# A recurrence, a mixture of experts and a feed-forward network in one kernel: the addition of an expert product's halves is issued one block later, and a split changes places with the next multiplication

## The chip, the core and the metric

The kernel runs on one core of one Trainium2 chip. The metric is device time in microseconds (us), from the first to the last instruction of one execution with what lies around it. The engines that matter here are PE (TensorE, the matrix multiplications, which write to the accumulators in PSUM), ACT (ScalarE), DVE (VectorE), POOL (GpSimd) and SP, whose queue issues most transfers (DMA). Each engine takes its own instructions strictly in the order in which the program lists them; between engines they wait for each other by semaphores.

## What is computed

Three layers follow each other. The reference, cut to what the change touches:

```python
x = attn_out.reshape(3072, 384)            # a complex linear recurrence over 768 steps (not touched)
# mixture of experts: each token goes to one of 8 experts
for e in range(8):
    h = np.maximum(x[mask] @ w1[e], 0.0)   # 384 -> 1024
    out[mask] = gate_w[mask, None] * (h @ w2[e])   # 1024 -> 384
# feed-forward network on all tokens
h = x @ w_in                               # 384 -> 2048
g = h * (1.0 / (1.0 + np.exp(-1.702 * h)))
y = g @ w_out                              # 2048 -> 384
```

## The kernel before

The matrix products run in 16-bit pieces: each operand is split into a rounded 16-bit half and the 16-bit rest ("split" below), and a product is the sum of three partial products (high by high, high by low, low by high) in one PSUM accumulator.

**The experts** (`moe`). The tokens are sorted by expert into 26 blocks of 128. The hidden dimension of 1024 is cut into NQ = 4 quarters of 256, and the program runs over the quarters q = 0 to 3 and in each over the 26 blocks, 104 steps in all. One step (q, b) issues in this order:

- `gemm1(q, b)`: six matmuls into one accumulator `ph` (three buffers), 512 columns wide; its two column halves hold parts of the same product and have to be added. ACT copies the right half to the tile `h` (L1083, three buffers), and DVE adds the left half to it (L1084): the addition of the halves.
- `late(2)`: `turn` of the block two steps back (q, b-2). PE transposes its `h` into the accumulator `pt` (L1090, two buffers), ACT takes the positive part of it as the high half of `hT` (L1093), DVE makes the low half (L1094), and that frees `pt`. Then `gemm2` of the block four steps back: six matmuls into `py` (L1105), which DVE adds to `acc` (L1112; L1110 in the first quarter).
- a share of two background jobs, each cut into steps. `halves` loads and splits the weights of the quarter after (while quarter 0 runs, those of quarter 1, and so on): ACT scales and rounds them (L997, L999, L1002), POOL subtracts (L1000), in quarter 0 also DVE (L1004). `narrow` turns the last layer's 64-bit weights into two 16-bit halves, from quarter 1 on, 32 weight blocks in all: six steps a weight block, with DVE in most (L946, L947, L950, L961, L964, L967), ACT in one (L957), and a transfer of the result (wh<-w, L970) that has to be through before the next L957 may write the same tile.

In quarter 0 each step also transposes and splits the next token block (`split`, L1068 to L1070).

So with n the number of the step, PE's row of work is gemm1(n), turn(n-2), gemm2(n-4), gemm1(n+1). PE's turn(n-2) needs two things of DVE: the addition of block n-2, and the low half of block n-4, which frees `pt`. Both stand next to each other in DVE's row, first the addition, then the low half.

**The end of the experts.** After the last step the remaining blocks are taken out in pairs, mixed with the first steps of the next layer (`begun`).

**The feed-forward network** (`Ffn`). Six tiles t of 512 tokens. `up` runs over f = 0 to 15 (NF = 16): nine matmuls into the accumulator `fph` (L1289, three buffers), then ACT's sigmoid (L1292) and DVE's multiplication with it (L1293), which frees `fph` and gives the hidden value; then the split of the value before, f-1: ACT's copy to 16 bit (L1296) and the subtraction of it (L1298), on DVE, and for t < 3 with f divisible by 3 on POOL. `down` multiplies with the second weight matrix (L1309) and is issued for the first time after three `up`s: the order is up 0, up 1, up 2, down 0, up 3, down 1, up 4, down 2, up 5, down 3, down 4, down 5. Beside `up` run `prep` of the next tile (squares L1232, a few small DVE steps, transposes L1256, splits L1260 and L1261) and in the first tiles the rest of `narrow`, by 1.5 steps an f in tile 0, 2 in tile 1, 2.5 in tile 2.

Of the kernel before, what the change touches and what calls it, by code (L numbers as in the profile page):

```python
# [16 lines left out]
AF = mybir.ActivationFunctionType  # L17
# [991 lines left out]
def moe(tc, cst, rt, wp, st, we, yd, lo, hi, x, psum, w0=None, w64=None, wh=None, ffn=None):  # L1009
# [3 lines left out]
    with ExitStack() as c2:  # L1013
# [58 lines left out]
        def gemm1(q, b):  # L1072
            w = ws[q]
            if b not in reg:
                reg[b] = nc.tensor.value_load(rt.eid[0:1, b:b + 1], min_val=0, max_val=E - 1)
            e = reg[b]
            ph = ph_.tile([P, 2 * FQ], F32, tag="ph", name=f"ph{q}_{b}")
            for k in range(KD):
                o = k * 2 * FQ
                nc.tensor.matmul(ph, lhsT=xT[:, b - lo, 0, k, :], rhs=w[:, e, o:o + 2 * FQ], start=k == 0, stop=False)  # L1080
                nc.tensor.matmul(ph[:, :FQ], lhsT=xT[:, b - lo, 1, k, :], rhs=w[:, e, o:o + FQ], start=False, stop=k == KD - 1)  # L1081
            h = wk.tile([P, FQ], F32, tag="h", name=f"h{q}_{b}", bufs=3)
            nc.scalar.copy(h, ph[:, FQ:])  # L1083
            nc.vector.tensor_tensor(out=h, in0=ph[:, :FQ], in1=h, op=ALU.add)  # L1084
            return h

        def turn(q, b, h):
            pt = pt_.tile([P, KD, P], F32, tag="pt", name=f"pt{q}_{b}")
# [31 lines left out]
                pass  # L1120
        gen = iter(())
        split(lo)
        hs, hTs = [], []
        NP = 2 * F2 // P
        fw, done, loaded = [], [], []
        conv = begun = iter(())
# [15 lines left out]

        def late(n):
            while len(hs) > n:
                q, b, h = hs.pop(0)
                hTs.append((q, b, turn(q, b, h)))
            while len(hTs) > n:
                gemm2(*hTs.pop(0))

        for q, b in seq:  # L1150
# [11 lines left out]
            if q == 0 and b > lo:  # L1162
                split(b + 1)
            hs.append((q, b, gemm1(q, b)))
            if q == 0 and b == lo:
                split(b + 1)
            late(LAG)
# [24 lines left out]
        late(LAG // 2)  # L1192
        next(begun, None)
        while hs:
            q, b, h = hs.pop(0)
            hTs.append((q, b, turn(q, b, h)))
        next(begun, None)
# [3 lines left out]
class Ffn:  # L1201
# [77 lines left out]
    def up(s, t, x, gT, tmp):  # L1279
# [3 lines left out]
        for f in range(s.NF + 1):  # L1283
            if f < s.NF:
                ph = s.ph.tile([P, T], F32, tag="ph", name=f"fph{t}_{f}")
                i = 0
                for k in range(KD):
                    for a, b in ((0, 0), (0, 1), (1, 0)):
                        nc.tensor.matmul(ph, lhsT=s.wi[f][:, a, k, :], rhs=xT[b][:, k], start=i == 0, stop=i == 3 * KD - 1)  # L1289
                        i += 1  # L1290
                h = tmp[f % 3]
                nc.scalar.activation(h, ph, AF.Sigmoid, scale=sig)  # L1292
                nc.vector.scalar_tensor_tensor(out=h, in0=ph, scalar=GS, in1=h, op0=ALU.mult, op1=ALU.mult)  # L1293
            if f:
                h = tmp[(f - 1) % 3]
                nc.scalar.copy(gT[:, f - 1, 0], h)  # L1296
                e = nc.gpsimd if t < 3 and f % 3 == 0 else nc.vector
                e.tensor_tensor(out=gT[:, f - 1, 1], in0=h, in1=gT[:, f - 1, 0], op=ALU.subtract)  # L1298
            yield

    def down(s, t, x, gT, tmp):
# [373 lines left out]
```

## Time and profile before

| | us |
|---|---|
| three runs, median | 966.82 (962.73 to 970.6) |
| the profiled execution | 961.36, with a span of 959.5 from the first to the last instruction |
| recurrence and routing | 0 to about 295 of the span |
| experts, quarter 0 | about 295 to 365 |
| experts, quarters 1 and 2 | about 365 to 490 |
| experts, quarter 3 and the end | about 490 to 558 |
| feed-forward network | about 553 to the end; its weights' conversion ends at about 650, PE ends at 938 |

Busy over the span: PE 881.4 us (92%), DVE 627.7 (65%), ACT 533.8 (56%), POOL 265.0 (28%). The granted clock was 0.985 on average and 1.00 between 374 and 662 us.

How to read it: PE is busy nearly throughout, so what counts is its idle time and what ended it. A row of the list of waits says which instruction waited, for which engine and line, how long in total, how often and at most. A row of the timeline gives start and duration in us, the engine, the line, the operation, the tiles written and read, the shape, and in brackets the engine's idle time before it with what ended it.

### The profile page before, as it was taken

What the parts mean: (1) busy time and instruction counts of PE and PEld (TensorE: products, weight loads), DVE (VectorE), ACT (ScalarE), POOL (GpSimd) and SP (SyncE); (2) the same over time, 40 slices, a digit from 0 to 9 for tenths busy, and PEclk for the clock granted to TensorE, in tenths of its full rate; (3) what the DMA queues carried; (4) which work ended last, traced back from release to release, by engine and by line L of the source; (5) the groups of instructions that cost most, each with busy time, mean ns of one, the idle gap of its engine ahead of it and who ended that gap; (6) DMA issues with size and microseconds to landing.
All of it is one profiled execution on the core that took longest, in us unless ns stands there. A gap on an engine that the chain in (4) does not pass through costs nothing.

```text
span 959.5 us, 17255 instructions
## 1 busy us (share of the span) xinstructions
PE 881.4 (92%) x5980; PEld 576.4 (60%) x5980; DVE 627.7 (65%) x1378; ACT 533.8 (56%) x1053; POOL 265.0 (28%) x215
## 2 busy tenths in 40 slices
PE   2789998999977999988999989989999999999994
PEld 0678877888965666555556644435545556456662
DVE  4887989887876898988998669996063170440000
ACT  7898776876645886765753456765063360440000
POOL 1330444136405663433520123223110101001110
PEclk9899999999988999999999999999999999999998
DMA  7532432220824755645637332121010000000000
GB/s 262 174 132 68 150 124 64 97 84 19 275 75 122 203 162 156 203 128 176 207 120 224 116 125 74 59 84 31 28 42 9 26 1 17 17 10 25 25 25 20
DMA packets 40403, 94.99 MB, mean 99 GB/s; under 512 B 6545, under 2 KB 19346, under 8 KB 40306
## 3 DMA queue, kind: packets, MB, share of 16 engines
q1 hardware_dynamic: 35138, 77.87, 25.1%
q0 software_dynamic: 4736, 14.69, 5.1%
q8 instruction: 56, 0.92, 0.4%
q10 hardware_dynamic: 432, 1.18, 0.4%
q14 instruction: 41, 0.34, 0.1%
HBM read 74.84 MB, written 18.81 MB: 98 GB/s over the span
## 4 chain that ended last, share of the span: by engine, by line
PE 44%; DVE 13%; DMA 4%; issue 3%; ACT 3%; POOL 0%; DVEq 0%; POOLq 0%; ACTq 0%; SPq 0%
PE fpo L1309 19%; PE fph L1289 12%; PE py L1105 5%; PE ph L1080 4%; DMA wh<-w 3%; PE ph L1081 2%; DVE w L961 2%; DVE x L1293 2%; DVE acc L1112 2%; DVE h L1084 1%; PE pt L1090 1%; DVE hT L1094 1%; DVE w L967 1%; DVE w L964 1%; PE px L1068 1%
## 5 line engine op out<-in xcount | busy, mean ns | idle before, releaser
L1289 PE MATMUL fph<-fx,fw 128*128 128x512 f16 x864 | 192.2, 379 | 6.4 <-DVE x L1293 6.3
L1293 DVE SCALAR_TENSOR_TENSOR x<-fph,x 128x512 f32<-128x512 f32 x96 | 65.9, 688 | 129.8 <-ACT x L1292 128.1
L1289 PEld LDWEIGHTS <-fw 128*128 128x128 f16 x864 | 84.5, 98 | 104.9 <-issue 9.5
L1309 PE MATMUL fpo<-fw,gT 128*128 128x384 f16 x768 | 125.3, 326 | 0.0
L1105 PE MATMUL py<-w,hT 128*128 x624 | 118.0, 326 | 1.3
L1080 PE MATMUL ph<-w,x 128*128 x312 | 108.1, 381 | 2.1 <-DVE w L1536 1.9
L1313 ACT ACTIVATE x<-fpo,fsm 128x384 f32<-128x384 f32 x24 | 13.9, 581 | 167.5 <-PE fpo L1309 167.5
L1309 PEld LDWEIGHTS <-gT 128*128 128x128 f16 x768 | 75.1, 98 | 49.9
L1292 ACT ACTIVATE x<-fph,fsm 128x512 f32<-128x512 f32 x96 | 65.6, 685 | 50.4 <-PE fph L1289 37.4
L1000 POOL TENSOR_TENSOR w<-ws,w 128x768 f16<-128x768 f32 x40 | 68.2, 1705 | 85.3 <-ACT w L999 80.6
L1314 POOL DMA_INDIRECT out<-x,fto x24 | 23.2, 965 | 245.3 <-ACT x L1313 245.3
L1081 PE MATMUL ph<-w,x 128*128 x312 | 85.4, 274 | 2.6 <-DVE x L1070 2.5
L1105 PEld LDWEIGHTS <-hT 128*128 128x128 f16 x624 | 60.9, 98 | 32.7 <-issue 4.1
L1083 ACT COPY h<-ph 128x256 f32<-128x256 f32 x104 | 38.5, 370 | 57.9 <-PE ph L1081 52.9
L1309 PE MATMUL fpo<-fw,x 128*128 128x384 f16 x384 | 62.7, 326 | 0.0
L1084 DVE TENSOR_TENSOR h<-ph,h 128x256 f32<-128x256 f32 x104 | 43.5, 418 | 26.7 <-ACT h L1083 25.8
L518 PE MATMUL pt<-c,f 128*96 128x128 f32 x384 | 53.1, 280 | 6.6 <-DVE f L492 4.8
L1309 PEld LDWEIGHTS <-x 128*128 128x128 f16 x384 | 37.6, 98 | 25.0
L536 PE MATMUL pt<-zq,zk 96*128 96x128 f32 x384 | 50.3, 278 | 0.7 <-ACT zk L526 0.7
L518 PEld LDWEIGHTS pt<-c,f 128*96 128x96 f32 x384 | 42.3, 129 | 13.5 <-DVE f L492 8.0
L1080 PEld LDWEIGHTS <-x 128*128 128x128 f16 x312 | 30.6, 98 | 31.4 <-issue 2.4
L1090 PE MATMUL pt<-c,h 128*128 128x128 f32 x208 | 40.6, 277 | 8.8 <-DVE hT L1094 8.6
(238 smaller groups left out, 1762.0 us busy)
## 6 DMA issues: line engine op xcount, KB each, us to landing
ws<-in_we SPq DMA_DIRECT2D x61, 384.0 KB
w<-in_w SPq DMA_DIRECT2D x32, 384.0 KB
qk<-in_qk SPq DMA_DIRECT2D x6, 1152.0 KB
yd<-acc SPq DMA_DIRECT2D x26, 192.5 KB
xd<-row SPq DMA_DIRECT2D x6, 589.5 KB
ar<-in_ar SPq DMA_DIRECT2D x6, 576.0 KB
ai<-in_ai SPq DMA_DIRECT2D x6, 576.0 KB
v<-in_v SPq DMA_DIRECT2D x6, 576.0 KB
```

Source lines behind the costliest of these rows:

```text
L518: nc.tensor.transpose(pt[:2 * D, h, :], T[FF][:, k, j * H + 4 * i + h].rearrange("p i d -> p (i d)"), cst["ident"])
L536: nc.tensor.matmul(ps[:, h - 4 * i, :], lhsT=T[ZK][:, h, :], rhs=T[ZQ][:, h, :], start=True, stop=True)
L1000: nc.gpsimd.tensor_tensor(out=wv[:, :, 1, :], in0=sv, in1=wv[:, :, 0, :], op=ALU.subtract)
L1080: nc.tensor.matmul(ph, lhsT=xT[:, b - lo, 0, k, :], rhs=w[:, e, o:o + 2 * FQ], start=k == 0, stop=False)
L1081: nc.tensor.matmul(ph[:, :FQ], lhsT=xT[:, b - lo, 1, k, :], rhs=w[:, e, o:o + FQ], start=False, stop=k == KD - 1)
L1084: nc.vector.tensor_tensor(out=h, in0=ph[:, :FQ], in1=h, op=ALU.add)
L1090: nc.tensor.transpose(pt[:, j, :], h[:, j * P:(j + 1) * P], cst["ident"])
L1105: nc.tensor.matmul(py, lhsT=hT[:, hl, j, :], rhs=w[:, e, o + off:o + off + DM], start=i == 0, stop=i == n - 1)
L1289: nc.tensor.matmul(ph, lhsT=s.wi[f][:, a, k, :], rhs=xT[b][:, k], start=i == 0, stop=i == 3 * KD - 1)
L1292: nc.scalar.activation(h, ph, AF.Sigmoid, scale=sig)
L1293: nc.vector.scalar_tensor_tensor(out=h, in0=ph, scalar=GS, in1=h, op0=ALU.mult, op1=ALU.mult)
L1309: nc.tensor.matmul(po, lhsT=gT[:, f, a, g * P:(g + 1) * P], rhs=s.wo[f][:, b, :], start=i == 0, stop=i == 3 * s.NF - 1)
```

## The change

Two edits. In `gemm1` the addition of the halves is no longer issued; accumulator and tile go to a list `whole`, and a new function `add` issues the addition of the oldest entry. The step calls it after the next block's `gemm1`, before `late`. Where a block would be transposed before that, `add` is called first. In `Ffn.up` the split of f-1 now stands ahead of the sigmoid and the multiplication of f.

```diff
@@ gemm1
             nc.scalar.copy(h, ph[:, FQ:])
+            whole.append((ph, h))
+            return h
+
+        def add():
+
+            ph, h = whole.pop(0)
             nc.vector.tensor_tensor(out=h, in0=ph[:, :FQ], in1=h, op=ALU.add)
-            return h
@@ late
             while len(hs) > n:
+                if len(whole) == len(hs):
+                    add()
                 q, b, h = hs.pop(0)
                 hTs.append((q, b, turn(q, b, h)))
@@ the step
             hs.append((q, b, gemm1(q, b)))
+            if len(whole) > 1:
+                add()
@@ the end of moe
         while hs:
+            if len(whole) == len(hs):
+                add()
             q, b, h = hs.pop(0)
             hTs.append((q, b, turn(q, b, h)))
@@ Ffn.up
-                h = tmp[f % 3]
-                nc.scalar.activation(h, ph, AF.Sigmoid, scale=sig)
-                nc.vector.scalar_tensor_tensor(out=h, in0=ph, scalar=GS, in1=h, op0=ALU.mult, op1=ALU.mult)
             if f:
                 h = tmp[(f - 1) % 3]
                 nc.scalar.copy(gT[:, f - 1, 0], h)
                 e = nc.gpsimd if t < 3 and f % 3 == 0 else nc.vector
                 e.tensor_tensor(out=gT[:, f - 1, 1], in0=h, in1=gT[:, f - 1, 0], op=ALU.subtract)
+            if f < s.NF:
+                h = tmp[f % 3]
+                nc.scalar.activation(h, ph, AF.Sigmoid, scale=sig)
+                nc.vector.scalar_tensor_tensor(out=h, in0=ph, scalar=GS, in1=h, op0=ALU.mult, op1=ALU.mult)
             yield
```

The rows of PE, POOL and SP are the same before and after; only those of DVE and ACT change. The line numbers of the changed kernel differ: there the addition is L1090, the low half of `hT` L1099, the sum into `acc` L1117, the copy of the split L1304, its subtraction L1306, the sigmoid L1309, the multiplication L1310.

First place: DVE in quarter 2, around block 20 (`h_20` is the block's tile, `hT_18` the low half of block 18, `w_13` and `w_14` are tiles of `narrow`). Before:

```order
L961 SCALAR_TENSOR_TENSOR w_14_6998<-w_14_6900,w_14_6998 128x384
L1084 TENSOR_TENSOR h_20_7042<-ph_20_7035,h_20_7042 128x256
L1094 SCALAR_TENSOR_TENSOR hT_18_7048<-pt_18_7045,hT_18_7048 128x256
L1112 SCALAR_TENSOR_TENSOR acc_4377<-py_16_7051,rs_4379,acc_4377 128x384
L964 SCALAR_TENSOR_TENSOR w_13_7029<-w_13_6902,w_13_7029 128x384
L967 SCALAR_TENSOR_TENSOR w_14_6998<-w_14_6900,w_14_6998 128x384
L1084 TENSOR_TENSOR h_21_7071<-ph_21_7064,h_21_7071 128x256
L1094 SCALAR_TENSOR_TENSOR hT_19_7077<-pt_19_7074,hT_19_7077 128x256
```

After:

```order
L961 SCALAR_TENSOR_TENSOR w_14_6997<-w_14_6899,w_14_6997 128x384
L1090 TENSOR_TENSOR h_19_7010<-ph_19_7003,h_19_7010 128x256
L1099 SCALAR_TENSOR_TENSOR hT_18_7047<-pt_18_7044,hT_18_7047 128x256
L1117 SCALAR_TENSOR_TENSOR acc_4377<-py_16_7050,rs_4379,acc_4377 128x384
L964 SCALAR_TENSOR_TENSOR w_13_7028<-w_13_6901,w_13_7028 128x384
L967 SCALAR_TENSOR_TENSOR w_14_6997<-w_14_6899,w_14_6997 128x384
L1090 TENSOR_TENSOR h_20_7041<-ph_20_7034,h_20_7041 128x256
L1099 SCALAR_TENSOR_TENSOR hT_19_7076<-pt_19_7073,hT_19_7076 128x256
```

The addition of block 20 has moved from ahead of the low half of block 18 to behind it, the sum into `acc` and this step's share of `narrow`.

Second place: DVE at the end of the experts (`h_25` is the last block's tile, `fx` belongs to the next layer). Before:

```order
L1084 TENSOR_TENSOR h_25_7934<-ph_25_7927,h_25_7934 128x256
L1094 SCALAR_TENSOR_TENSOR hT_23_7940<-pt_23_7937,hT_23_7940 128x256
L1112 SCALAR_TENSOR_TENSOR acc_4377<-py_21_7943,rs_4379,acc_4377 128x384
L1261 SCALAR_TENSOR_TENSOR fx_1_7635<-fpt_2_7920,fsi_7741,fx_0_7634 128x512
L1094 SCALAR_TENSOR_TENSOR hT_24_7957<-pt_24_7954,hT_24_7957 128x256
L1112 SCALAR_TENSOR_TENSOR acc_4377<-py_22_7960,rs_4379,acc_4377 128x384
L1112 SCALAR_TENSOR_TENSOR acc_4377<-py_23_7969,rs_4379,acc_4377 128x384
L1094 SCALAR_TENSOR_TENSOR hT_25_7981<-pt_25_7978,hT_25_7981 128x256
```

After, from the same low half of block 23 on:

```order
L1099 SCALAR_TENSOR_TENSOR hT_23_7939<-pt_23_7936,hT_23_7939 128x256
L1117 SCALAR_TENSOR_TENSOR acc_4377<-py_21_7942,rs_4379,acc_4377 128x384
L1272 SCALAR_TENSOR_TENSOR fx_1_7634<-fpt_2_7919,fsi_7740,fx_0_7633 128x512
L1099 SCALAR_TENSOR_TENSOR hT_24_7956<-pt_24_7953,hT_24_7956 128x256
L1117 SCALAR_TENSOR_TENSOR acc_4377<-py_22_7959,rs_4379,acc_4377 128x384
L1117 SCALAR_TENSOR_TENSOR acc_4377<-py_23_7968,rs_4379,acc_4377 128x384
L1090 TENSOR_TENSOR h_25_7933<-ph_25_7926,h_25_7933 128x256
L1099 SCALAR_TENSOR_TENSOR hT_25_7981<-pt_25_7978,hT_25_7981 128x256
```

The addition of block 25 now stands behind the sums of blocks 22 and 23, right ahead of the low half of its own block.

Third place: DVE in tile 1 of the feed-forward network, from f = 3 to f = 6 (the subtractions are the rows that write `gT`; that of f = 5 is on POOL). Before:

```order
L1293 SCALAR_TENSOR_TENSOR x<-fph_3_8382,x 128x512
L946 TENSOR_SCALAR w_25_8399<-w_25_8342 128x384
L947 TENSOR_SCALAR w_25_8399<-w_25_8399 128x384
L950 TENSOR_SCALAR w_25_8399<-w_25_8399 128x384
L1293 SCALAR_TENSOR_TENSOR x<-fph_4_8404,x 128x512
L1298 TENSOR_TENSOR gT_8024<-x,gT_8024 128x512
L1236 TENSOR_REDUCE fsm_8337<-fsm_8337 128x1
L961 SCALAR_TENSOR_TENSOR w_25_8399<-w_25_8342,w_25_8399 128x384
L964 SCALAR_TENSOR_TENSOR fw<-w_24_8344,fw 128x384
L1293 SCALAR_TENSOR_TENSOR x<-fph_5_8422,x 128x512
L1298 TENSOR_TENSOR gT_8024<-x,gT_8024 128x512
L967 SCALAR_TENSOR_TENSOR w_25_8399<-w_25_8342,w_25_8399 128x384
```

After, from the same row on:

```order
L1310 SCALAR_TENSOR_TENSOR x<-fph_3_8382,x 128x512
L946 TENSOR_SCALAR w_25_8399<-w_25_8342 128x384
L947 TENSOR_SCALAR w_25_8399<-w_25_8399 128x384
L950 TENSOR_SCALAR w_25_8399<-w_25_8399 128x384
L1306 TENSOR_TENSOR gT_8024<-x,gT_8024 128x512
L1310 SCALAR_TENSOR_TENSOR x<-fph_4_8404,x 128x512
L1247 TENSOR_REDUCE fsm_8337<-fsm_8337 128x1
L961 SCALAR_TENSOR_TENSOR w_25_8399<-w_25_8342,w_25_8399 128x384
L964 SCALAR_TENSOR_TENSOR fw<-w_24_8344,fw 128x384
L1306 TENSOR_TENSOR gT_8024<-x,gT_8024 128x512
L1310 SCALAR_TENSOR_TENSOR x<-fph_5_8422,x 128x512
L967 SCALAR_TENSOR_TENSOR w_25_8399<-w_25_8342,w_25_8399 128x384
```

Each subtraction on DVE now stands ahead of the multiplication that it followed; on ACT, in the same way, the copy of f-1 stands ahead of the sigmoid of f, where it stood behind it.

## Rows read from the trace of the kernel before

**Rows 1.** Waits of PE: who waited, for whom: us in total, times, longest us.
```profile
PE pt L1090 <- DVE hT L1094: 8.6, 10, 1.9
PE fph L1289 <- DVE x L1293: 6.3, 7, 1.6
```

**Rows 2.** Timeline, quarters 0 to 3: gemm2 of three steps on PE.
```profile
365.59 1.14 PE L1105 MATMUL py<-w,hT 128*128 x6
367.76 1.14 PE L1105 MATMUL py<-w,hT 128*128 x6
...
487.29 0.97 PE L1105 MATMUL py<-w,hT 128*128 x5
```

**Rows 3.** Stretches: length, then busy us of PE, PEld, DVE, ACT, POOL, granted clock.
```profile
374.00:432.00 58.00, 54.09 (x337) 32.92 (x336) 52.50 (x115) 40.70 (x87) 27.60 (x16) 1.00 0.53 166
594.00:625.00 31.00, 29.78 (x144) 14.02 (x143) 29.84 (x64) 23.26 (x45) 9.26 (x9) 1.00 0.28 86
```

**Rows 4.** Timeline, quarter 2, after ACT had waited for weights: ACT, DVE.
```profile
439.72 0.35 ACT L1083 COPY h<-ph 128x256 f32<-128x256 f32 x1
439.97 0.39 ACT L1093 ACTIVATE hT<-pt 128x256 f16<-128x256 f32 x1
...
440.11 0.42 DVE L1084 TENSOR_TENSOR h<-ph,h 128x256 f32<-128x256 f32 x1 [3.84 <-ACT h L1083]
```

**Rows 5.** Timeline, quarter 2, the last of the ten waits for pt: DVE, PE.
```profile
483.82 0.41 DVE L1094 SCALAR_TENSOR_TENSOR hT<-pt,hT 128x256 f16<-128x256 f32 x1
...
484.15 0.60 DVE L1112 SCALAR_TENSOR_TENSOR acc<-py,rs,acc 128x384 f32<-128x384 f32 x1
484.29 0.44 PE L1090 MATMUL pt<-c,h 128*128 128x128 f32 x2 [0.80 <-DVE hT L1094]
...
484.68 0.90 DVE L964 SCALAR_TENSOR_TENSOR w<-w,w 128x384 f16<-128x384 f32 x1
...
485.50 0.55 DVE L967 SCALAR_TENSOR_TENSOR w<-w,w 128x384 int32<-128x384 int32 x1
...
485.97 0.41 DVE L1084 TENSOR_TENSOR h<-ph,h 128x256 f32<-128x256 f32 x1
...
489.23 0.38 PE L1090 MATMUL pt<-c,h 128*128 128x128 f32 x2
```

**Rows 6.** Timeline, end of the experts: the last transposition and the sum behind gemm2.
```profile
553.42 0.38 PE L1090 MATMUL pt<-c,h 128*128 128x128 f32 x2
553.62 0.62 DVE L1112 SCALAR_TENSOR_TENSOR acc<-py,rs,acc 128x384 f32<-128x384 f32 x1 [0.32 <-PE py L1105]
```

**Rows 7.** Timeline, ACT in tile 0 of the feed-forward network: copy, then sigmoid.
```profile
572.21 0.61 ACT L1296 CAST x<-x 128x512 f16<-128x512 f32 x1
...
572.72 0.69 ACT L1292 ACTIVATE x<-fph,fsm 128x512 f32<-128x512 f32 x1
```

**Rows 8.** Timeline, tile 1, multiplications of f = 3 to 6 on DVE, one copy.
```profile
602.68 0.68 DVE L1293 SCALAR_TENSOR_TENSOR x<-fph,x 128x512 f32<-128x512 f32 x1
...
604.71 0.68 DVE L1293 SCALAR_TENSOR_TENSOR x<-fph,x 128x512 f32<-128x512 f32 x1
605.31 0.68 DVE L1298 TENSOR_TENSOR gT<-x,gT 128x512 f16<-128x512 f32 x1
605.42 0.62 ACT L1296 CAST gT<-x 128x512 f16<-128x512 f32 x1 [0.28 <-DVE x L1293]
...
606.91 0.69 DVE L1293 SCALAR_TENSOR_TENSOR x<-fph,x 128x512 f32<-128x512 f32 x1
...
608.58 0.69 DVE L1293 SCALAR_TENSOR_TENSOR x<-fph,x 128x512 f32<-128x512 f32 x1
```

**Rows 9.** Chain of work that ended last, tile 5: sixteen times nine matmuls.
```profile
821.34 31.08 PE fph L1289 x144
```

**Rows 10.** Timeline, one step of narrow on DVE beside a subtraction on POOL, and without.
```profile
592.65 1.15 POOL L1298 TENSOR_TENSOR x<-x 128x512 f16<-128x512 f32 x1 [4.56 <-ACT x L1296]
592.82 1.39 DVE L961 SCALAR_TENSOR_TENSOR w<-w,w 128x384 int32<-128x384 int32 x1
...
600.08 0.55 DVE L961 SCALAR_TENSOR_TENSOR w<-w,w 128x384 int32<-128x384 int32 x1
```

**Rows 11.** Timeline, PE's waits at the start and the end of tile 1.
```profile
597.75 1.46 PE L1289 MATMUL fph<-fx,fw 128*128 128x512 f16 x6 [0.78 <-DVE x L1293]
...
625.77 0.59 PE L1289 MATMUL fph<-fx,fw 128*128 128x512 f16 x2 [0.21 <-DVE x L1293]
```

More of the change, by code (lines that the diff above doesn't have):

```diff
@@ L1122, in moe @@
         split(lo)
-        hs, hTs = [], []
+        hs, hTs, whole = [], [], []
         NP = 2 * F2 // P
```

## The prediction

> **What bounds the kernel now.** I read PE's waits first, then the stretches in which they lie, then single steps of the timeline, and the chain of work last. PE is busy 92% of the span, so a change can only move what PE waits for. Two of its waits touch the edits [rows 1]: the transposition's accumulator `pt`, released by DVE's low half of `hT` (8.6 us, ten waits), and the feed-forward accumulator `fph`, released by DVE's multiplication (6.3 us, seven waits). The first lies in quarters 1 and 2: a step of PE takes 2.17 us (367.76 − 365.59), and 49 steps lie between the first and the last of the three rows, so 49 × 2.17 = 106.3 us would do and 121.7 went: 15.4 us were lost there [rows 2]. In that time DVE is nearly as busy as PE, 52.5 of 58 us against 54.1, ACT 40.7; in tile 1 of the feed-forward network DVE has 29.84 of 31 us against PE's 29.78 [rows 3]. So these are the two stretches where DVE's order decides. In tile 5, with no `narrow` beside it, PE runs on its own: 31.08 us for 16 f, 1.94 us an f [rows 9]. I expect nothing from the recurrence, quarter 3 and tiles 3 to 5.
>
> **Edit 1, the addition one block later.** It removes no instruction. What it could free is DVE: the addition waits for ACT's copy (3.84 us of idle ahead of it in one place), and what stands behind it in DVE's row waits as well. But right behind it stands the low half of `hT`, and that needs ACT's positive part, which stands right behind the same copy in ACT's row [rows 4]. There the copy starts at 439.72, the addition at 440.11; the positive part ends at 440.36, so without the addition in front the low half could start at about 440.40, against about 440.45 behind it (start to start of the pair in [rows 5]: 484.15 − 483.82 = 0.33). The gain is some 0.05 us an event. I count 0.
>
> What it costs: PE's turn(n−2) needs the addition of that block and, for `pt`, the low half of the block two before. Before, both stood side by side in DVE's row. Now the addition comes a DVE step later, behind the low half, the sum into `acc` and that step's `narrow`. At the last of the ten waits [rows 5] the low half ends at 484.23 and PE starts at 484.29. DVE then does the sum (to 484.75), L964 (to 485.58), L967 (to 486.05) and the next addition (to 486.38); in the new order that slot holds the addition this turn needs. So it starts at about 486.38 + 0.06 = 486.44 instead of 484.29, 2.15 us later. A part comes back: from 484.29 to the turn two steps on (489.23) went 4.94 us where two periods are 4.34. The 0.60 was paid by two turns that had to wait, 0.30 each. After the change only the first of them is late, and I take 2.15 − 0.30 = **+1.8 us**. I count it once, not per wait: when DVE and ACT come to a place in these quarters is set by their own work and by transfers that do not move, so each wait's release moves by the same step and PE is behind by the same amount all the way. Bounds: 0, if PE still had a step in hand; +0.85 if only the sum and the addition (0.52 + 0.33, start to start) lie between; +3.2 if a slow step of `narrow` lies between (L961 took 1.39 beside POOL, 0.55 alone [rows 10]; 2.15 + 0.84 = 3.0, and 0.2 more).
>
> In quarter 0 I count 0. There DVE's split of the next token block stands just ahead of the addition, and PE's next `gemm1` needs that split already; the turn stands behind this `gemm1`, which covers the 0.33 us of the addition. Without that cover it would be one step, 2.2 us, once.
>
> At the end of the experts the addition of block 25 now stands behind the sums of blocks 22 and 23. The last of these ends at 553.62 + 0.62 = 554.24 [rows 6]; 0.33 for the addition and 0.05 for the signal give 554.62. The last turn started at 553.42: **+1.2 us**, between 0.9 and 1.4, as nothing else is left on PE ahead of it.
>
> **Edit 2, the split ahead of the multiplication.** Write M(f) for the multiplication, S(f) for the subtraction. Before, ACT's sigmoid of f needed only PE, and the copy of f−1 came behind it. Now sigmoid(f) stands behind copy(f−1), which needs M(f−1), and M(f) needs sigmoid(f). That is a closed chain from one multiplication to the next: M 0.69, signal 0.03 (605.39 to 605.42 [rows 8]), copy to sigmoid 0.51 from start to start, sigmoid 0.69 [rows 7], signal 0.03: 1.95 us, against PE's 1.94. On its own that is harmless. But DVE in tiles 0 to 2 doesn't work evenly: it falls behind on f's with much `narrow` and catches up on light ones, and the chain is now a floor under the light ones.
>
> Tile 1 shows the cycle of three [rows 8]: 602.68 to 604.71 is 2.03 us, to 606.91 2.20, to 608.58 1.67; together 5.90, or 1.97 an f, just above PE's 1.94. In the new order the work between two multiplications is another: each S on DVE slides ahead of its M, 0.6 us. The f with `narrow`'s three steps gets 2.03 + 0.60 = 2.63, the next stays at 2.20, and the light f, whose S is on POOL, keeps 0.60 + 0.47 = 1.07 us of DVE work, but the chain holds it at 1.96. The cycle takes 2.63 + 2.20 + 1.96 = 6.79 instead of 5.90: 0.89 us idle on DVE per light f. Between PE's two waits at 597.75 and 625.77 [rows 11] lie 28.0 us or 14 f, with four or five cycles; the three `fph` buffers and DVE's own waits on PE take up some, and I count three: 3 × 0.89 = **+2.7 us**. In tile 0 the first wait finds an S of 0.6 ahead of its M, and `prep`'s squares on ACT come between copy and sigmoid and stretch the chain: **+1.5** (0 to 2). In tile 2 `narrow` gives DVE more work every f than the chain takes: **+0.3**. Together +4.5, between 0 and +7 (5 cycles in tile 1, 2 in tile 0 and half a microsecond in tile 2). In tiles 3 to 5 chain and PE differ by 0.01 to 0.02 us an f, 0.3 a tile, which the buffers hide.
>
> **A gain that the new order could give.** POOL's subtraction began beside DVE's L961, and this took 1.39 us where 0.55 is usual [rows 10]. After the swap POOL's subtraction starts about half a microsecond behind M(f−1)'s end and lies beside the next multiplication, which reads PSUM and one tile in SBUF. I counted six long steps of this kind between 562 and 650 us; six times 0.84 is 5 us of DVE time at most. I left it out of the sum since the L961 lies at the same place in the row and may meet POOL's conversions instead.
> The Trainium skill, *SBUF — State Buffer*, section "Who interferes with whom", says that a DVE instruction with two SBUF inputs contends with a GpSimd instruction that reads SBUF, because they share a read port, and that one with at most one SBUF input does not. L961 has two such inputs, so the rows agree; by the rule alone the multiplication would not suffer and the second rival below gains weight.
>
> **Sum.** 1.8 + 1.2 + 4.5 = +7.5 us. The profiled execution took 961.36, so 968.9; the median of the three runs lies 5.5 us above that execution (966.82), hence **974.3 us**.
>
> **Rivals.**
> - *Only the experts pay* (+3.0, 969.8 us): the feed-forward network breaks even, as the freed contention pays for the floor. For it: S done while DVE would wait, and the 0.84 us of [rows 10]. Against it: DVE has only 1.2 us of 31 idle in tile 1 [rows 3], so there is little waiting to fill.
> - *Faster*: the seven waits for `fph` vanish because POOL's subtraction no longer meets L961. −6.3 + 1.2, with edit 1 otherwise neutral: 966.82 − 5.1 = 961.7 us. It decides if copy(f−1) is done before PE ends f, so that sigmoid(f) never waits; against it stands that M(f−1) itself is late where PE waits.
> - *Worse, a new wait*: turn(n−1) now needs the addition at the head of the DVE step that comes right behind the low half of block n−3, so a two-step loop closes over turn, positive part, low half, sum, `narrow`, addition: 0.44 + 0.39 + 0.41 + 0.52 + 0.33 + two steps of `narrow` (0.9 + 0.5) = 3.5 of 4.34 us. With a slow `narrow` step (+0.84) it is full, and then each of the ten waits grows by up to 1 us beside terms above at their upper ends: +12 to +18, about 982 us.
> - *Nothing measurable*: buffers cover both edits, 966.8 us.
>
> **How the numbers follow.** Chances: forecast (+5 to +12, 972 to 979) 0.48; only the experts 0.20; faster 0.12; worse 0.12; nothing 0.08. The range goes from 965, which leaves out most of the faster case, to 982, which leaves out half of the worse one. One per cent, 9.7 us, is about what a measurement of this kernel can tell from no change. Above 976.5 lie the worse case and a third of the forecast (0.12 + 0.16, and 0.02 of the rest): slower 0.30. Below 957.2 only a part of the faster case: 0.03. Within 1%: 0.67.
>
> **What would show it.** Right, step by step: PE's waits for `pt` are released by the addition of DVE (tile `h`) instead of `hT`, and are larger in total; the gemm2 that stood at 487.29 lies about 1.8 us further from the one at 365.59; the last turn of the experts waits about 1.2 us for an addition behind a sum into `acc`; in tiles 0 to 2 the waits for `fph` grow from 6.3 to about 11 us, and DVE idles before multiplications on ACT's sigmoid in light f's, whose 1.67 us become about 1.96. Wrong: `fph` waits that shrink while sigmoids wait for nothing (the faster case); waits for `pt` that grow by far more than 2 us in total, with the addition as releaser at most of them (the worse case); a stretch of tiles 3 to 5 that gets longer, which no step here allows for.

## The result, and the profile after

The changed kernel takes 975.76 us (median of four runs, 971.35 to 979.42), the kernel before 967.87 (four runs): ratio 1.0104, 95% interval 1.0061 to 1.0147, so 6 to 14 us slower. The prediction said 974.3, in a range of 965 to 982. The profiled execution took 971.35 with a span of 969.6; the old one had 961.36 and 959.5, so it is 10.0 us longer (10.1 from span to span) where the sum said 7.5. Executions of one kernel spread over some 10 us, and in the traces most of this lies ahead of the experts, where no edit reaches (step 26 of the table below begins between 368 and 379 us), which is why the table counts from that step.

PE's waits in the changed kernel (who waited, for whom: us in total, times, longest us), against 8.6 and 6.3 in [rows 1]:

```profile
PE pt L1095 <- DVE h L1090: 14.4, 13, 3.8
PE fph L1300 <- DVE x L1310: 7.8, 9, 1.9
PE fpt L1267 <- DVE fx L1272: 1.5, 3, 0.5
```

The turns now wait for the addition (tile `h`) instead of the low half, and for 5.8 us more (1.0 of them is the last turn of the experts). The waits for `fph` have grown by 1.5 only; 1.5 us of waits for the next tile's preparation are new.

To see where the time goes I follow one instruction through all kernels: ACT's positive part behind the turn of step n (n counts the 104 steps; 26 is the first of quarter 1, 52 of quarter 2, 103 the last). Its start at steps 26 and 74, before and after (timeline: start, duration, engine, line):

```profile
370.19 0.38 ACT L1093 ACTIVATE hT<-pt 128x256 f16<-128x256 f32 x1
...
489.70 0.39 ACT L1093 ACTIVATE hT<-pt 128x256 f16<-128x256 f32 x1
```

```profile
369.18 0.38 ACT L1098 ACTIVATE hT<-pt 128x256 f16<-128x256 f32 x1
...
492.98 0.39 ACT L1098 ACTIVATE hT<-pt 128x256 f16<-128x256 f32 x1
```

From 26 to 74 went 119.51 us before and 123.80 after: 4.29 us lost in quarters 1 and 2, where the prediction had 1.8. In the same way the first sigmoid of a tile gives the loss in the feed-forward network; the column "tile 1" is thus what tile 0 has cost. One execution of each kernel, us behind the kernel before, counted from step 26 (steps) and from step 103 (tiles); "long steps" are DVE steps of `narrow` of over 1 us in quarters 1 and 2:

| kernel | step 52 | 53 | 74 | 103 | tile 1 | tile 2 | tile 3 | long steps |
|---|---|---|---|---|---|---|---|---|
| before | 0 | 0 | 0 | 0 | 0 | 0 | 0 | 8 |
| changed | 3.9 | 2.5 | 4.3 | 6.3 | 1.3 | 4.7 | 4.6 | 12 |
| e1 edit 1 alone | 4.3 | 2.9 | 5.9 | 7.1 | 0.0 | 0.0 | 0.1 | 13 |
| e2 edit 2 alone | -0.1 | -0.3 | -0.3 | -0.3 | 1.3 | 4.7 | 4.7 | 9 |
| e3 DVE half of edit 2 | -0.5 | -0.8 | 0.9 | 0.9 | 0.2 | 3.3 | 3.6 | 10 |
| e4 ACT half of edit 2 | -0.3 | -0.3 | 0.7 | 0.7 | 3.7 | 5.0 | 6.9 | 9 |
| e5 behind the low half | 0.1 | 0.1 | 3.6 | 3.7 | 0.5 | 0.2 | 0.3 | 15 |
| e6 behind `acc` | 0.3 | -0.1 | 0.6 | 1.0 | -0.5 | -0.4 | -0.3 | 9 |
| e7 quarter 1 alone | 4.3 | 2.7 | 2.4 | 2.4 | -0.4 | -0.4 | -0.2 | 12 |
| e8 POOL's f alone | 0.0 | 0.1 | 0.4 | 0.4 | 1.1 | 1.2 | 1.3 | 8 |
| e9 quarter 2 alone | 0.5 | -0.1 | 3.2 | 3.2 | 0.3 | 0.3 | 0.4 | 13 |
| e10 as e5, more POOL | 0.0 | 0.1 | 3.9 | 4.3 | 0.6 | 3.6 | 4.3 | 13 |
| e11 no POOL subtraction | -6.2 | -7.7 | -13.6 | -13.4 | 0.3 | 0.3 | 0.3 | 0 |
| e12 the same, edit 1 | -6.2 | -7.7 | -11.9 | -10.5 | -0.5 | -0.5 | -0.4 | 0 |

Parts that a kernel does not change lie within 0.9 us of zero; that is how far a single number carries. In tiles 4 and 5 the changed kernel stays at 4.6 and 4.9. Quarter 0 gave it 0.8, but there one gap of 1.3 us (step 12) is in some executions and not in others, with either order. So the 10.1 us of the span are −1.0 up to step 26, +4.3 in quarters 1 and 2, +0.8 in quarter 3 (none in e1, so not shown to be the edit's), +1.3 at the end of the experts, +4.6 in the feed-forward network up to tile 3 and 0.2 behind it.

At the waits of quarters 1 and 2 the changed kernel shows this (POOL's subtraction for the next quarter's weights, a step of `narrow` on DVE, the addition, PE):

```profile
417.45 1.64 POOL L1000 TENSOR_TENSOR w<-ws,w 128x768 f16<-128x768 f32 x1 [0.36 <-ACT w L999]
417.56 1.95 DVE L961 SCALAR_TENSOR_TENSOR w<-w,w 128x384 int32<-128x384 int32 x1
...
419.90 0.41 DVE L1090 TENSOR_TENSOR h<-ph,h 128x256 f32<-128x256 f32 x1
...
420.45 0.41 PE L1095 MATMUL pt<-c,h 128*128 128x128 f32 x2 [2.10 <-DVE h L1090]
...
443.07 1.64 POOL L1000 TENSOR_TENSOR w<-ws,w 128x768 f16<-128x768 f32 x1 [21.60 <-ACT w L999]
443.09 2.03 DVE L961 SCALAR_TENSOR_TENSOR w<-w,w 128x384 int32<-128x384 int32 x1
...
445.60 0.58 PE L1095 MATMUL pt<-c,h 128*128 128x128 f32 x2 [3.77 <-DVE h L1090]
...
483.39 1.88 DVE L961 SCALAR_TENSOR_TENSOR w<-w,w 128x384 int32<-128x384 int32 x1
...
485.20 0.41 DVE L1090 TENSOR_TENSOR h<-ph,h 128x256 f32<-128x256 f32 x1
...
485.75 0.41 PE L1095 MATMUL pt<-c,h 128*128 128x128 f32 x2 [0.72 <-DVE h L1090]
```

The addition stands behind a step of `narrow` that takes 1.9 to 2.0 us beside POOL, where [rows 10] has 0.55 alone. And behind two of these waits the clock falls. Stretches of 2 us (length, busy us of PE, PEld, DVE, ACT, POOL, granted clock, DMA share, GB/s):

```profile
418.00:420.00 2.00, 0.35 (x3) 0.00 (x0) 2.00 (x3) 1.66 (x5) 1.63 (x2) 1.00 0.00 0
420.00:422.00 2.00, 1.55 (x10) 0.99 (x11) 2.00 (x5) 0.38 (x1) 1.47 (x1) 0.95 0.27 98
422.00:424.00 2.00, 2.00 (x9) 1.26 (x8) 1.97 (x6) 0.31 (x1) 0.00 (x0) 0.50 0.53 143
424.00:426.00 2.00, 2.00 (x10) 1.01 (x9) 0.78 (x3) 0.86 (x3) 0.00 (x0) 0.69 0.16 62
```

0.50 is the lower level, 1.2 GHz; the three lower rows give (0.05 + 0.50 + 0.31) × 2 = 1.7 us of matmul time lost. The same happens behind the wait of 3.77 us. The kernel before had no fall in quarters 1 and 2. How much of this matmul time the kernel really loses is another question; e2 and e6 below bear on it.

At the end of the experts the last turn stands where the prediction put it, behind the sum and the addition, as against [rows 6]:

```profile
557.65 0.62 DVE L1117 SCALAR_TENSOR_TENSOR acc<-py,rs,acc 128x384 f32<-128x384 f32 x1 [0.27 <-PE py L1110]
558.18 0.41 DVE L1090 TENSOR_TENSOR h<-ph,h 128x256 f32<-128x256 f32 x1
...
558.65 0.44 PE L1095 MATMUL pt<-c,h 128*128 128x128 f32 x2 [1.04 <-DVE h L1090]
```

In tile 1 the light f, 1.67 us in [rows 8], now takes 611.15 − 609.20 = 1.95 and 617.59 − 615.63 = 1.96; DVE stands idle for 0.81 us until ACT's sigmoid, which started behind the copy:

```profile
609.20 0.69 DVE L1310 SCALAR_TENSOR_TENSOR x<-fph,x 128x512 f32<-128x512 f32 x1
...
609.91 0.62 ACT L1304 CAST gT<-x 128x512 f16<-128x512 f32 x1 [0.34 <-DVE x L1310]
...
610.44 0.68 ACT L1309 ACTIVATE x<-fph,fsm 128x512 f32<-128x512 f32 x1
...
611.15 0.69 DVE L1310 SCALAR_TENSOR_TENSOR x<-fph,x 128x512 f32<-128x512 f32 x1 [0.81 <-ACT x L1309]
...
615.63 0.69 DVE L1310 SCALAR_TENSOR_TENSOR x<-fph,x 128x512 f32<-128x512 f32 x1
...
617.59 0.69 DVE L1310 SCALAR_TENSOR_TENSOR x<-fph,x 128x512 f32<-128x512 f32 x1 [0.81 <-ACT x L1309]
```

The largest single piece of tile 1 is another one, at its start. ACT waits there for a transfer, does the next tile's squares and a step of `narrow`, and only then the copy; in the new order DVE's subtraction and multiplication wait behind that copy. From the tile's first multiplication to its second go 607.06 − 603.64 = 3.42 us; before it was 598.87 − 597.01 = 1.86, since no copy stood in that multiplication's way:

```profile
604.88 0.49 ACT L1243 ACTIVATE fps<-fr 128x384 f32<-128x384 f32 x1 [1.28 <-DMA fr<-yd,sidx]
...
605.82 0.60 ACT L1304 CAST gT<-x 128x512 f16<-128x512 f32 x1
...
606.45 0.69 DVE L1306 TENSOR_TENSOR gT<-x,gT 128x512 f16<-128x512 f32 x1 [0.85 <-ACT gT L1304]
607.06 0.68 DVE L1310 SCALAR_TENSOR_TENSOR x<-fph,x 128x512 f32<-128x512 f32 x1
```

### The profile page after: what moved, and what is told of

Its sections match the earlier page's. It is cut to its first block, busy times and chain, and to the rows that moved or that the text cites. A ratio compares the mean times of both kernels' runs of the same rounds, so it can differ in the third digit from the quotient of the medians.

```text
span 969.6 us, 17347 instructions
## 1 busy us (share of the span) xinstructions
PE 885.3 (91%) x5980; PEld 578.0 (60%) x5980; DVE 625.5 (65%) x1378; ACT 536.5 (55%) x1053; POOL 264.7 (27%) x215
## 4 chain that ended last, share of the span: by engine, by line
PE 45%; DVE 12%; ACT 4%; issue 3%; DMA 3%; POOL 0%; ACTq 0%; DVEq 0%; POOLq 0%; SPq 0%
PE fpo L1321 19%; PE fph L1300 11%; PE py L1110 6%; PE ph L1080 4%; PE ph L1081 2%; DVE w L961 2%; DVE x L1310 2%; PE pt L1095 2%; DVE acc L1117 1%; DMA wh<-w 1%; DVE hT L1099 1%; DVE gT L1306 1%; ACT x L1309 1%; DVE w L964 1%; PE px L1068 1%
## 5 line engine op out<-in xcount | busy, mean ns | idle before, releaser
L1310 DVE SCALAR_TENSOR_TENSOR x<-fph,x 128x512 f32<-128x512 f32 x96 | 65.8, 685 | 109.0 <-ACT x L1309 108.8
L1309 ACT ACTIVATE x<-fph,fsm 128x512 f32<-128x512 f32 x96 | 65.5, 683 | 13.3 <-DMA out<-x,fto 5.9
L1304 ACT CAST gT<-x 128x512 f16<-128x512 f32 x64 | 39.4, 616 | 40.2 <-DVE x L1310 40.2
L1099 DVE SCALAR_TENSOR_TENSOR hT<-pt,hT 128x256 f16<-128x256 f32 x104 | 43.3, 416 | 25.5 <-ACT hT L1098 25.2
L1321 PEld LDWEIGHTS <-x 128*128 128x128 f16 x384 | 37.6, 98 | 25.0
L1306 DVE TENSOR_TENSOR gT<-x,gT 128x512 f16<-128x512 f32 x54 | 37.3, 690 | 23.4 <-ACT gT L1304 18.0
```

The source lines that it names most:

```text
L1099: nc.vector.scalar_tensor_tensor(out=hT[:, 1], in0=pv, scalar=0.0, in1=hT[:, 0], op0=ALU.max, op1=ALU.subtract)
L1321: nc.tensor.matmul(po, lhsT=gT[:, f, a, g * P:(g + 1) * P], rhs=s.wo[f][:, b, :], start=i == 0, stop=i == 3 * s.NF - 1)
```

## The experiments

The theory: edit 1 costs because a turn's addition comes a DVE step later, edit 2 because the sigmoid behind the copy holds light f's at 1.96 us. Rivals stand in each expectation. The edits are shown in short, not as the lines stand in the kernels.

**The edits apart: e1 and e2.** Each is the diff above without the other edit.

> Only edit 1 (the addition one block later); the feed-forward network as before. The trace of the changed kernel lies 5.3 us behind the old one at the experts' last transposition: 1.0 us gained in quarter 0, 4.3 lost in quarters 1 and 2, 0.8 in quarter 3, 1.2 at the end. If the two edits are independent, this kernel is 5 us slower (ratio 1.005), with the feed-forward network's multiplications 4.5 to 5.5 us later throughout and its 6.3 us of waits for fph unchanged. Rival: the feed-forward network takes the lateness up, since it is DVE and its conversions that limit there, and not when PE came: then the offset shrinks to below 2 us by tile 2 and the ratio is below 1.002.

> Only edit 2 (the split ahead of the multiplication); the experts as before. Theory of the floor (sigmoid behind copy): offset 0 at the first multiplication, some 6 us at the end of tile 2, flat in tiles 3 to 5; ratio 1.005 to 1.006. Rival: most of the 5.9 us in the changed kernel came from the experts' late end (conversions bunched behind it), and edit 2 by itself costs under 3 us, ratio below 1.003.

e1: 968.47 us, ratio 1.0052 (1.0014 to 1.0090); e2: 970.41 us, 1.0028 (0.9997 to 1.0058). In e1 the offset of 7.1 us stays through all tiles; in e2 the experts are level and 4.7 us arise in tiles 0 and 1. The edits add up, 7.1 + 4.7 against 6.3 + 4.6 in the changed kernel, and neither takes up the other. The 2.7 us of e2's ratio are less than its trace shows, within its interval; the 5.0 us of e1's ratio likewise.

**The halves of edit 2: e3 and e4.**

```diff
 # e3, f-loop: ACT in the old order, DVE in the new
+sigmoid(f)
 copy(f-1)
 subtract(f-1)
-sigmoid(f)
 multiply(f)
 # e4: ACT in the new order, DVE in the old
 copy(f-1)
-subtract(f-1)
 sigmoid(f)
 multiply(f)
+subtract(f-1)
```

> Half of edit 2: on DVE the subtraction of f-1 stands ahead of the multiplication of f, on ACT sigmoid and copy stay in their old order. Theory of the floor: the sigmoid needs PE alone again, the light f (its subtraction on POOL) can catch up, the cycle of three takes 5.9 us as before, and the cost is under 1.5 us (ratio 1.000 to 1.0015). Rival, the slide: what costs is that each fph is freed 0.6 us later behind a subtraction; then it costs as much as all of edit 2, 5 to 6 us (ratio 1.005 to 1.006).

> The other half of edit 2: on ACT the copy of f-1 stands ahead of the sigmoid of f, on DVE multiplication and subtraction stay in their old order. Theory of the floor: light f's are held at about 1.96 us, but the heavy ones do not get 0.6 longer, so 0.3 us a cycle in tile 1 and some more in tile 0 where the squares stand between copy and sigmoid: 2 to 3 us (ratio 1.002 to 1.003), DVE idle ahead of multiplications on ACT's sigmoid. Rival, the slide: nothing (ratio 1.000).

e3: 967.92 us, 1.0005 (0.9975 to 1.0035); e4: 974.14 us, 1.0072 (1.0040 to 1.0104). DVE's multiplications in tiles 0 to 2 (groups of instructions: busy us, mean ns of one, idle us just before them and what ended it), before, changed, e3, e4:

```profile
L1293 DVE SCALAR_TENSOR_TENSOR x<-fph,x 128x512 f32<-128x512 f32 x48 | 32.8, 685 | 8.7 <-ACT x L1292 7.6 <-ACT fps L1232 0.9
```

```profile
L1310 DVE SCALAR_TENSOR_TENSOR x<-fph,x 128x512 f32<-128x512 f32 x48 | 32.9, 686 | 14.2 <-ACT x L1309 14.1
```

```profile
L1303 DVE SCALAR_TENSOR_TENSOR x<-fph,x 128x512 f32<-128x512 f32 x48 | 32.8, 684 | 3.4 <-ACT x L1293 3.3
```

```profile
L1299 DVE SCALAR_TENSOR_TENSOR x<-fph,x 128x512 f32<-128x512 f32 x48 | 33.0, 688 | 17.6 <-ACT x L1296 16.6 <-ACT gT L1293 0.7
```

Where the sigmoid stands behind the copy DVE waits 14 to 17 us for it, where it does not, 3 to 8. So the floor is ACT's order. But its size is not what I expected: e4 loses 6.9 us up to tile 3, not 2 to 3, and more than all of edit 2 (4.7). A part of that is in tile 0, where the old order let DVE catch up behind a long interval with 0.60 and 1.25 us from one multiplication to the next (569.24 to 569.84, 581.34 to 582.60); in e4 the same two take 1.95 and 1.96. The DVE half gives about 2 us back when it is added. I put that down to the meeting with POOL, since of the long steps of `narrow` in tiles 0 to 2 (six before, five in e4, four in e3) one is left with all of edit 2; this is argued from the counts and not shown by a run. In e3 the light f's take 1.07 us, with no floor; its 3.6 us come for the most part with one stall, the one at the start of tile 1 again, 2.5 us here. ACT waited for a transfer and did the next tile's squares, the copy came late, DVE's subtraction waited for it and the multiplication behind that:

```profile
609.26 0.60 ACT L1296 CAST gT<-x 128x512 f16<-128x512 f32 x1
...
609.90 0.69 DVE L1300 TENSOR_TENSOR gT<-x,gT 128x512 f16<-128x512 f32 x1 [1.97 <-ACT x L1293]
610.50 0.69 DVE L1303 SCALAR_TENSOR_TENSOR x<-fph,x 128x512 f32<-128x512 f32 x1
...
611.24 1.24 PE L1289 MATMUL fph<-fx,fw 128*128 128x512 f16 x3 [2.26 <-DVE x L1303]
```

and the clock fell behind it, 1.7 us of matmul time:

```profile
610.00:612.00 2.00, 0.76 (x3) 0.36 (x3) 2.00 (x4) 1.73 (x5) 0.00 (x0) 0.87 0.39 99
612.00:614.00 2.00, 2.00 (x7) 0.63 (x6) 2.00 (x5) 1.57 (x5) 0.00 (x0) 0.50 0.00 0
614.00:616.00 2.00, 2.00 (x9) 0.86 (x8) 1.93 (x4) 1.84 (x5) 1.42 (x2) 0.78 0.47 175
```

So the rival of the slide is right to a part: a subtraction ahead of the multiplication hands on a delay of the copy. The size is that of one execution: e3's ratio gives 0.5 us and at most 3.4.

**How far the addition is moved: e5 and e6.**

```diff
 # e5: behind the turn, ahead of gemm2's sum
 turn(n-2)
+add(n)
 gemm2(n-4)
 # e6: behind gemm2's sum, ahead of narrow
 gemm2(n-4)
+add(n)
 narrow
```

> The addition of a block moves behind the low half of hT only: the same step, ahead of the sum into acc and of narrow; the feed-forward network as before. A turn needs the addition of its block and the low half of two blocks before, which stand side by side in both orders. Theory (what costs is what stands between the two): no loss, the positive part of hT at the end of quarter 2 within 0.7 us of the old kernel counted from the end of quarter 0, ratio 1.000; PE's waits for pt stay near 8.6 us. Rival (any addition behind the low half costs, since DVE then waits for ACT's positive part with the addition still to do): 3 us or more, as in the run with edit 1 alone, ratio 1.003 to 1.005.

> The addition of a block moves behind the low half and the sum into acc, still ahead of this step's narrow; the feed-forward network as before. Theory (the price of a late release is the DVE work in between): 0.52 + 0.33 = 0.85 us later at the end of quarter 1 and again at the end of quarter 2, so 0.8 to 1.8 us behind the old kernel at the end of quarter 2, against 5.7 to 5.9 with edit 1 alone; nothing at the end of the experts. Rival (the clock that fell behind PE's longer waits made most of the loss in edit 1): a loss only if the granted clock falls in quarters 1 or 2, and then 1.6 us for each fall.

e5: 970.94 us, 1.0021 (0.9983 to 1.0059); e6: 965.72 us, 1.0001 (0.9959 to 1.0043). e6 behaves nearly as the theory said (0.6 us, a little below the 0.8). Its rival, the clock, does not hold as it stood: the clock fell once in e6 (at 448 us) and the 1.6 us did not follow. The same is to be seen in e2, where nothing of the experts was changed: behind a wait of 1.79 us the clock fell,

```profile
442.00:444.00 2.00, 2.00 (x8) 0.76 (x6) 2.00 (x4) 2.00 (x6) 1.69 (x2) 0.50 0.14 34
```

and at step 74 e2 is level with the kernel before, which had no fall. So a fall alone does not make the loss of edit 1; beside longer waits of PE it may add to it.

e5 is level until step 70 and then loses 3.5 us up to step 74, which the theory does not allow. There, between 478 and 496 us, five long steps of `narrow` follow each other, two of them here:

```profile
486.68 1.64 POOL L1000 TENSOR_TENSOR w<-ws,w 128x768 f16<-128x768 f32 x1 [1.77 <-ACT w L999]
486.81 1.73 DVE L947 TENSOR_SCALAR w<-w 128x384 f32<-128x384 f32 x1
...
492.94 2.05 POOL L1000 TENSOR_TENSOR w<-ws,w 128x768 f16<-128x768 f32 x1 [1.91 <-ACT w L999]
...
493.41 1.99 DVE L967 SCALAR_TENSOR_TENSOR w<-w,w 128x384 int32<-128x384 int32 x1
```

L947 takes 0.36 where POOL is not at work. It was not this one execution: e10 has the same experts, is 0.4 us behind at step 70 and 3.9 at step 74. So a small shift in DVE's row (the 0.3 us of one addition) goes with other steps meeting POOL, 15 and 13 long ones instead of 8, and with a loss of more than ten times the shift.

**Edit 1 in one quarter: e7 and e9.** `add` is issued late only where q is 1 (e7) or 2 (e9):

```diff
-            if len(whole) > 1:
+            while len(whole) > (q == 1):
                 add()
```

> The addition one block later in quarter 1 alone; quarters 0, 2, 3 and the feed-forward network as before. Theory (the lead is lost at the end of each of the two quarters, and what quarter 1 loses goes on through the weight transfers that are issued behind it): 2 to 3 us behind at block 1 of quarter 2 and the same 2 to 3 us at the end of quarter 2, half of what edit 1 loses in both. Rival (the loss is paid once, as the prediction had it, at the last wait, in quarter 2): the 2 to 3 us are given back in quarter 2, within 0.7 us of the old kernel at its end.

> The counterpart of the run with quarter 1 alone: the addition one block later in quarter 2 only, the rest and the feed-forward network as before. Theory (lost anew in each quarter): nothing until the weights' transfer at block 1 of quarter 2, then 1.8 us at its end, up to 3.4 if the granted clock falls behind a wait there and the old kernel's did not; with the 2.4 us of quarter 1 this makes the 4.3 to 5.9 of edit 1. Rival (the loss is one for both quarters): the same 2.4 us as with quarter 1 alone or nothing, so that the two runs do not add up.

e7: 966.87 us, 0.9991 (0.9953 to 1.0028); e9: 970.44 us, 1.0004 (0.9964 to 1.0044). The timed ratios cannot tell 3 us; the offsets can. e7 loses 4.3 us in quarter 1, gets 1.6 back at the weights' transfer and keeps 2.4. That the transfers moved can be read directly: the first weights for the quarter after are issued 64.7 us behind step 26 in the kernel before (434.92 − 370.19) and 67.7 in e7 (445.37 − 377.67). e9 loses nothing until there and then 3.2. Together 5.6, as e1's 5.9: the loss arises in each quarter, not once. Each shows one fall of the clock; e9's, the longer one, comes with a wait of 4.54 us.

**Edit 2 for POOL's f alone: e8, and more subtractions for POOL: e10.**

```diff
 # e8: only where t < 3 and f % 3 == 0
+copy(f-1); POOL subtract(f-1)
 sigmoid(f); multiply(f)
 # e10 (experts as e5)
-e = nc.gpsimd if t < 3 and f % 3 == 0 else nc.vector
+e = nc.gpsimd if t < 3 and f % 3 != 1 else nc.vector
```

> Edit 2 only for the f whose subtraction POOL does (every third in the first three tiles): ACT's copy ahead of the sigmoid there, everything else in the old order; the experts as before. Theory of the floor: these f's are the light ones, so they are held at 1.96 us as with all of edit 2, but the heavy ones do not get 0.6 longer; long steps of narrow beside POOL (1.4 to 1.5 us) go away as with all of edit 2: between 1 us faster and 2 us slower (ratio 0.999 to 1.002), against 4.7 us of loss in the feed-forward network with all of edit 2. Rival (the floor alone makes the loss, the slide nothing): 4 to 5 us slower, ratio 1.004 to 1.005.

> Two parts that do not touch each other. Experts: the addition behind the low half of hT once more, whose first run was level up to block 14 of quarter 2 and then lost 3.3 us where late weight transfers and long steps of narrow came together. Theory (that was this one execution): within 0.7 us at the end of quarter 2. Rival (the order costs there): 3 us again. Feed-forward network: old order, but POOL takes two subtractions of three instead of one in the first three tiles. If DVE's work is what PE waits for, 5 subtractions of 0.6 us less a tile take 2 to 4 us off the 6.3 of waits for fph; rival: POOL's 1.15 us and the steps of narrow that it holds up eat this, and the network is level or up to 3 us slower.

e8: 969.49 us, 0.9996 (0.9958 to 1.0033); e10: 973.07 us, 1.0047 (1.0009 to 1.0085). e8's network is 1.3 us behind at tile 3, with a fall of the clock at 577 to 581. That is within what the theory allowed, and the rival, 4 to 5 us from the floor alone, falls. But the long steps beside POOL did not go (five are left), so I was wrong on what takes them away. In tile 1 e8 holds its light f's at 1.95 us (610.29 to 612.24) as the changed kernel does, and the next two take 1.75 and 2.20; the cycle of three stays at 5.90, as before. So under POOL's f's alone the floor costs nothing there: the f behind gives back what the light one loses. e10 answers its first question (above); its network loses 4.3 us, more than the rival said, with a fall of the clock of its own at 584. Neither is a better kernel.

**No subtraction on POOL: e11 and e12.** For the weights of quarters 2 and 3 POOL writes zeros, so this part of the computation is left out:

```diff
-nc.gpsimd.tensor_tensor(out=low, in0=sv, in1=high, op=ALU.subtract)
+nc.gpsimd.memset(low, 0.0)        # q > 1 only
```

> The kernel before, but in quarters 1 and 2 POOL no longer subtracts for the next quarter's weights: it writes zeros in the place of their low halves (that part of the computation is left out). It is the base for the next run. Expected by either theory: the long steps of narrow in these quarters (3 to 4 a quarter of over 1 us, where 0.36 to 0.56 is usual) fall to none or one, PE's 8.6 us of waits for pt shrink, and the time falls by 1 to 5 us.

> The same with edit 1 (the addition one block later), the feed-forward network as before; POOL's subtraction for the weights left out in quarters 1 and 2 in the same way. With POOL's subtraction edit 1 cost 5.9 us up to the end of quarter 2, and two more long steps of narrow stood in each quarter. Theory (what costs is PE's lead, a DVE step a quarter, and the clock that falls behind the longer waits): against the base without the subtraction still 2.5 to 5 us at the end of quarter 2. Rival (what costs is that the moved steps of narrow meet POOL's subtraction more often): under 1.5 us. At the end of the experts 1.2 us more by both.

e11: 946.79 us, ratio 0.9862 (0.9808 to 0.9917); e12: 956.26 us, 0.9896 (0.9860 to 0.9933). By its ratio e11 is 13 us faster, where I had expected 1 to 5. No long step is left, and PE's waits for `pt` in quarters 1 and 2 are, in e11 and in e12 (8.6 before):

```profile
PE pt L1093 <- DVE hT L1097: 0.7, 2, 0.5
```

```profile
PE pt L1098 <- DVE h L1093: 3.0, 2, 2.4
```

Edit 1 costs nothing in quarter 1 here (both are at −6.2 at step 52), 2.3 us of waits in quarter 2, of which 1.6 are left at step 74, and 1.2 more at the end. That is between the two expectations and is the size that the prediction had for a lead lost once (1.8). The other 2.7 to 4.3 us of the changed kernel and of e1 are there only with POOL's subtraction. Leaving it out takes away the long steps, the falls of the clock and the longer work of POOL together, so it does not tell which of them makes those us.

## Why the prediction was right, and where it was not

- *The result*: right, 975.76 for 974.3, slower by 1.0% with an interval that reaches from 0.6 to 1.5. That it came within 1.5 us is in part luck: from trace to trace 10.1 us went and not 7.5, and the medians of four runs differ by 7.9.
- *What is gained by edit 1 (0.05 us an event, counted 0)*: right; no kernel with a later addition is ahead at step 74.
- *Edit 1 in quarters 1 and 2, +1.8, "I count it once, not per wait"*: this step failed in its size; 4.3 us went in the changed kernel and 5.9 in e1, both above the upper bound of 3.2. The reason given, that "transfers do not move", is wrong: e7 shows that 2.4 us of quarter 1's loss go on, since the weights of the quarter after are issued behind it, and e9 that quarter 2 loses again. The price of one such loss came out right where POOL's subtraction was left out (1.6, e12 against e11). With it, the addition stands behind a step of `narrow` that takes 1.9 us or more; I had that as the upper bound, +3.2, and should have taken it, as such a step lies at the longest waits. Even the bound was short, since it took 1.39 us from tile 0; in quarters 1 and 2 the kernel before already had L961 at 1.91 to 2.00 us beside POOL (at 418.1 and 441.7 us). Besides, 12 or 13 long steps are met instead of 8, and the clock falls twice, which by e2 and e6 need not cost anything of itself. Over all runs with POOL's subtraction the loss at step 74 goes with the count of long steps (8 to 10: at most 0.9 us; 12 to 15: 2.4 to 5.9). How much of a loss is lead, long step and clock was not separated any further.
- *The end of the experts, +1.2*: right. From step 102 to 103 the offset grows by 1.3 us in the changed kernel and in e1, and not at all in e5 and e7.
- *The chain of 1.95 us*: right, to 0.01. The sum of +4.5 for the feed-forward network: 4.6 (tile 0 1.3 for 1.5; tile 1 3.3 for 2.7; tile 2 0.0 for 0.3). But its inside was not right, and the agreement is luck. In tile 1, multiplication by multiplication, the four light f's give +1.2 us and the four heavy ones +1.7 (they took 2.27 and 2.93 us, not 2.63 throughout), where "three cycles" of 0.89 were counted; the start of the tile gives +1.6, which the sum didn't have; and a long step of `narrow` that is gone gives −1.0. ACT's order by itself costs 6.9 (e4), and what DVE's order then gives back, about 2 us, is the gain that I left out of the sum. Errors of both signs offset each other.
- *The gain by POOL*: the multiplications, with one input in PSUM and one in SBUF, kept their mean (685 ns before, 686 changed), and the steps of `narrow` with two SBUF inputs took up to 2.0 us beside POOL's subtraction and 0.55 to 0.56 beside e11's writes of zeros. But L947, with one SBUF input, took 1.73 us beside the subtraction (e5) and 0.36 without, and up to 0.85 in e11. The Trainium skill, *SBUF — State Buffer*, section "Who interferes with whom", excepts from the rule that the prediction cites instructions in a mode that uses both ports; it says that a `tensor_scalar`, as L947 is, can enter such a mode and contend with GpSimd. It also says that a GpSimd instruction that only writes does not contend with the second input of a two-input one. The traces agree with both.
- *Signs*: the releaser of `pt`, the last turn, the 1.96 us and the level tiles 3 to 5 came as said. The gemm2 that stood at 487.29 lies 4.3 us further from the one at 365.59 and not 1.8 (490.56 − 364.58 = 125.98, before 121.70). The waits for `fph` are 7.8 and not 11; PE's recorded waits in the tiles grew by about 3 us, 1.5 of them for the preparation of the next tile, and some 1.4 of the 4.6 us stand in no recorded wait.
- *The rivals*: the one of the feed-forward network at break-even and the faster one fell with e2's tiles. The worse one named slow steps of `narrow` as its trigger and waits for `pt` that grow by far more than 2 us as its sign; both came (4.8 us more in quarters 1 and 2, the addition as releaser at all twelve), but took the experts 2.5 us beyond the forecast, not 5 to 10, and whether its two-step loop was ever full was not looked at by a run of its own.

## What to carry to other kernels

An instruction that is moved back behind a neighbour's work can cost that work as it is at the worst place, not at the mean one; look there first for what lengthens it. When two instructions on one engine change places, draw the closed chain from one use of a buffer to the next and compare it with the period of the bounding engine: 1.95 against 1.94 us told here where time would go, though not how much: that depended on whether the work behind could catch up, and on a late transfer ahead of one copy. And a loss is paid once only if nothing behind it moves; a transfer that is issued in order behind the late engine carries it on.

## What the chip showed beside that

POOL's subtraction in quarters 1 and 2 costs this kernel far more than its place off the critical path suggests: without it the span is 14.9 us shorter (944.6 for 959.5), 13.6 of them between steps 26 and 74, where 7.9 stand in PE's recorded waits for `pt`. DVE's long steps beside it take 1.1 to 2.0 us instead of 0.36 to 0.56. The granted clock is 1.00 there in both kernels, so the clock isn't what makes the difference. POOL's own work is shorter too (0.79 us a write of zeros, 1.72 a subtraction), and what that alone brings was not separated. It is a hint of what a version that keeps the two apart could gain; none was tried that computes everything.

A wait of PE can cost more than itself: behind waits of 2.1 and 3.8 us the granted clock stood at 0.50 for some 3 us, 1.7 us of matmul time each time (with the 4.54 us of e9 for longer). The length of the wait alone does not tell: behind 1.94 us in the kernel before it stayed at 1.00, and behind 2.39 us in e12 too, while in e2 it fell behind 1.79 at the place of the 1.94. And not every fall reaches the end: e2 had one and was level some 20 steps later.
